# The 26 block products of the last group also for the group before it, its early sums on another engine, and some work around groups 0 and 1 moved

## The chip, the core and the metric

The kernel runs on one core of a Trainium2 chip. A core has five engines that each run their own list of instructions in order and wait for each other by semaphores: TensorE (PE in the profile: matmuls, with the weight loads of each shown apart as PEld), VectorE (DVE), ScalarE (ACT), GpSimd (POOL) and SyncE (SP), which here only issues DMAs, as POOL does in a few places. SBUF is the on-chip memory in which the operands lie, PSUM the banks that matmuls write, HBM the memory outside. The metric is the device time of one execution in microseconds (us). One execution was also taken by the hardware profiler; all views below are of that one.

## The reference

Everything is fp32. Attention in chunks of 64 tokens, then a layer that adds the real part of a two-dimensional Fourier transform, normalises each token, and sends it through two weight matrices, 512 to 2048 and back:

```python
# q, k, v: (8 batches, 8 heads, 576 tokens, 64)
scores = scale * np.matmul(q_c, k_c.transpose(0, 1, 2, 4, 3))     # per chunk of 64
attn = softmax(scores)
x = (attn @ v_c) -> (8, 576, 512)
u = x + np.real(np.fft.fft(np.fft.fft(x, axis=1), axis=2))
un = (u - mean(u)) / np.sqrt(var(u) + 1e-06)
ch = np.maximum(un @ w_ch1, 0.0) @ w_ch2                        # 512 -> 2048 -> 512
out = u + ch
```

## The kernel before

**Tiles and groups.** The 4608 tokens lie in 36 tiles of 128 rows. They are of three kinds: LO and HI, whose chunks are mirror images of each other in the Fourier step, and RE ("rest"), the odd chunks of two batches. Four tiles are a group, and there are nine: groups 0 to 7 are the LO and HI tiles of one batch each, group 8 is the four rest tiles. A group passes through an up phase (512 to 2048, with relu) and a down phase (2048 to 512, and u is added). Between the matmuls of one group stand, as side work, attention and Fourier of a later batch (`side`, L1487), and the normalising (`normed`, L983), transposing (`turned`, L1001) and combining (`combined`, L1019) of the next group's tiles.

**Fewer matmuls by sums of blocks.** Group 0 is computed plainly (`up_first` L1187, `down_plain` L1231: 64 matmuls of 128x512 in each phase). From group 1 on (`up_halves` L1266, `down_halves` L1320) each matrix product is cut into 2 x 2 x 2 blocks and made from seven block products in place of eight, whose operands are sums of blocks: 7 x 2 x 8 = 112 matmuls of 128x256 in a down phase. `combined` makes the sums of un, `operands` (L1167) those of the hidden values h1 for the down phase: two on VectorE and one on GpSimd for each of eight m, issued in the up phase behind the pair that made them. Group 8's down phase (`down_few`, L1386) is cut finer, into 4 x 4 x 2 blocks, and made from 26 products (the table PRODUCTS) of four matmuls of 128x256, 104 in all. Its first operands are sums of 128x512 blocks of h1, on GpSimd: the six of the list EARLY while the up phase is in its third pair of four, the others in down_few, next to the product that they follow (`sums`, L1180). It reads each product's result out of PSUM on VectorE.

**Sums of weights.** These are made once on the chip and kept in HBM. Up phases read s1 in slabs of 256 KB (ring of 10, L1157); halved down phases read s2 in slabs of 1 MB (ring of 3 in the tile wb, L1162); down_few reads 0.5 MB blocks, some of s2, most of s3 (L1160). s3 holds 19 sums. `make_rest` (L1110) makes them: for each of two halves it loads eight blocks (L1126), makes 23 sums of 128x512 on GpSimd (L1135) and stores 19 (L1142), in buffers that attention and Fourier need no longer. The main loop starts it when group 6 is in its down phase, takes the first real step five steps later, and leaves out every fourth step from group 7 on. A ring of 11 slabs for s3 is filled from two steps into group 8's up phase.

**Order.** All code stands under `tc.manual_schedule()`: every engine executes its instructions in the order in which the program text issues them. The main loop calls a step t of the running phase's generator, and then of the side work that is due by a count (`begin[g]`, `ready_at[g]`: the step in which group g+1's values must be there). An up phase of groups 1 to 8 has 16 steps, a down phase 14, down_few 13. SP's DMAs are issued in program order too. `FEW` (L1149) is the first group that uses down_few.

**Around groups 0 and 1.** In down_plain, the four tiles of group 1 are normed after m = 10, 10, 12, 12 and turned after m = 12, 13, 14, 14 of 16; the combined sums (L1028 to L1030) follow in the same step. At the end VectorE adds u to each result (L1251). Beside this, Fourier of batch 1 runs its last three mixes (L842), one of them for the rest rows. A mix goes to a bank of the tag "pt" (two of them), which the transposes use as well; the last mix of batch 1 goes to the tag "att" (one), which scores (`sc`, L449) use. VectorE reads a mix in L852 and L853.

Of the kernel before, what the change touches and what calls it, by code (L numbers as in the profile page):

```python
# [8 lines left out]
FP32 = mybir.dt.float32  # L9
# [7 lines left out]
def kernel(  # L17
# [32 lines left out]
    nc = tc.nc  # L50
# [3 lines left out]
    CH = 64  # L54
    NC = S // CH
    NM = 2
# [10 lines left out]
    G = 2 * NM  # L67
# [4 lines left out]
    one_p = ctx.enter_context(tc.tile_pool(name="one", bufs=1))  # L72
# [79 lines left out]
        "s24=s10-sb22", "s22=w-s10", "s25=w+s4", "s1=b21-s4", "s17=b21+b41", "s18=b12+b32", "s12=s18-s17", "s6=b42-s18",  # L152
    )
    STORED = tuple(text.split("=")[0] for text in MADE if text[0] == "s")
    NR2, NS3 = len(PRODUCTS), 11
    s3 = dram.tile([len(STORED), 128, Z3], FP32, name="s3")
    slab3 = [wb[:, i * Z3:(i + 1) * Z3].rearrange("p (m e) -> p m e", m=4) for i in range(6)]

# [634 lines left out]
    def fourier(b):  # L793
# [25 lines left out]
            yield  # L819
            z_joined()  # L820
        nc.scalar.copy(zs[0][0:1, 2], middle)
        if h == 1:
            z_rest(h)
        for i in range(NM):
            z_tile(zf, i)
        if h == 0:
            z_rest(h)
        yield

        def mixed(i):  # L830
            if (b, i) == (1, NM - 1):
                mix = ps_a.tile([128, 2, 512], FP32, tag="att", name="mix")[:, 0]
            else:
                mix = ps_t.tile([128, 512], FP32, tag="pt", name="mix")
            zt = zr.rearrange("p t h f -> p t (h f)") if i == NM else zf[:, :, 128 * i:128 * (i + 1)]
            for T, (cols, tab) in enumerate((
                (slice(0, HM + 1, 2), ce),
                (slice(1, HM, 2), co),
                (slice(0, DM, 2), cx),
                (slice(HM + 1, DM, 2), so),  # L840
            )):
                nc.tensor.matmul(  # L842
                    out=mix[:, cols], lhsT=zt[:, T], rhs=tab,
                    start=(T == 0), stop=(T == 3), skip_group_check=True,
                )
# [12 lines left out]
            eng = nc.gpsimd if kind(n) == HI else nc.vector  # L858
            eng.tensor_tensor(out=x[:, 0:w], in0=y[:, 0:w], in1=x[:, 0:w], op=ALU.add)

        for i in ((NM,) if h == 1 else ()) + tuple(range(NM)):
            y = both(*mixed(i))
            ns = [rests[b // 2]] if i == NM else [at[LO, b, i], at[HI, b, i]]
            for n in ns:
                added(y, n)
            means(ns)
            yield

    def fourier_early():
# [78 lines left out]
        for i in range(NM):  # L948
# [13 lines left out]
            if i == 0:  # L962
                normed(0, 1)
                turned(0, 0)
                keep_warm(1)
        put_off[2]()
        columns(1)
        normed(0, 2)
        turned(0, 2)
# [64 lines left out]
    def store(n, o):  # L1034

        last = n in groups[-1][1::2]
        for h, (b, c) in enumerate(chunks(n)):
            r0, t0 = h * CH, c * CH
            if kind(n) == LO:
                to = out[b, t0 + 1:t0 + CH + 1, :][::-1].rearrange("(i r) d -> r i d", r=2)[::-1]  # L1040
                nc.gpsimd.dma_start(out=to, in_=o[r0:r0 + CH])  # L1041
            elif kind(n) == RE:
                eng = nc.scalar if last and h else nc.sync
                eng.dma_start(out=out[b, t0 + 1:t0 + CH:2, :], in_=o[r0:r0 + ODD])
                eng.dma_start(out=out[b, t0 + 4:t0 + CH:2, :], in_=o[r0 + ODD + 2:r0 + CH])
                eng.dma_start(out=out[b, 0:t0 + 3:t0 + 2, :], in_=o[r0 + ODD:r0 + ODD + 2])
            else:
                for r in range(2):
                    nc.sync.dma_start(out=out[b, t0 + 1 - r:t0 + CH:2, :], in_=o[r0 + ODD * r:r0 + ODD * r + ODD])


# [58 lines left out]
    def make_rest():  # L1110
# [3 lines left out]
        z, spare = Z3 // 2, []  # L1114
        for i in range(4):
            spare.append(xall[:, 2 * G:2 * G + 4, :].rearrange("p a f -> p (a f)")[:, i * z:(i + 1) * z])
        for tag, n in (("q", 2), ("k", 2), ("zf", 2), ("two", 1), ("qT", 1), ("kT", 1), ("pT", 1)):
            t = one_p.tile([128, n * z], FP32, tag=tag, name="part")
            spare += [t[:, i * z:(i + 1) * z] for i in range(n)]
        last = {x: i for i, text in enumerate(MADE) for x in text.replace("=", "-").replace("+", "-").split("-")}  # L1120
        for half in range(2):
            part = slice(half * z, (half + 1) * z)
            where, behind = {}, []
            for name in ("b31", "b41", "b42", "b11", "b32", "d", "w", "b21"):
                where[name] = spare.pop(0)
                nc.sync.dma_start(out=where[name], in_=block_of(name)[:, part])  # L1126
                if half and name in ("b41", "b11", "d"):
                    yield
            yield
            for i, text in enumerate(MADE):  # L1130
                name = text.split("=")[0]
# [8 lines left out]
                while behind and (len(behind) > 3 or i == len(MADE) - 1):  # L1140
                    old = behind.pop(0)
                    nc.sync.dma_start(out=block_of(old)[:, part], in_=where[old])  # L1142
                    if last[old] <= i and old not in done_with:
                        done_with.append(old)
                spare += [where[x] for x in done_with if x not in behind]
                if i % 2:
                    yield

    FEW = NG - 1  # L1149
    first_of = {1: 1, 2: 1}  # L1150
    n_slab = {1: 0, 2: 0, 3: 0}

# [24 lines left out]
            return yall[:, i + 1].rearrange("p (m t) -> p m t", m=4)  # L1177
        return h1[:, 4 * j:4 * j + 4, i * 128:(i + 1) * 128]

    def sums(h1, texts):  # L1180

        for text in texts:
            out_, a, b, op = parsed(text)
            out_, a, b = (block_a(h1, x) for x in (out_, a, b))
            nc.gpsimd.tensor_tensor(out=out_, in0=a, in1=b, op=op)

    def up_first():  # L1187

# [42 lines left out]
    def down_plain(g, h1):  # L1231
# [4 lines left out]
        for m in range(KF):  # L1236
# [14 lines left out]
                    nc.vector.tensor_tensor(out=o, in0=dn, in1=natural(n), op=ALU.add)  # L1251
                    store(n, o)
            for j in range(G):
                if m == (10, 10, 12, 12)[j]:
                    normed(g + 1, j)
                if m == (12, 13, 14, 14)[j]:
                    turned(g + 1, j)
                    if j >= 2 and g + 1 >= first_of[1]:
                        joined.append((g + 1, j - 2))
# [6 lines left out]
    def up_halves(g):  # L1266
# [7 lines left out]
        for pair in range(HF // 2):  # L1274
            pas, pbs = {}, {}
            for turn_, o in enumerate(UP):
# [161 lines left out]
    with tc.manual_schedule():  # L1438
# [79 lines left out]
        for g in range(NG):  # L1518
            for _ in mlp(g):
# [108 lines left out]
```

## Time and profile before

| | us |
|---|---|
| runs | 1069.3, 1070.77, 1072.9 (median 1070.77) |
| profiled execution | 1069.92 |
| its span in the profile | 1068.1 |
| mean granted TensorE clock | 0.997 of full |

The times in the timeline count from the start of the span. In it, the phases begin on PE at:

| group | up phase | down phase |
|---|---|---|
| 0 | 52.0 | 115.8 |
| 1 | 192.5 | 252.0 |
| 2 | 310.2 | |
| 6 | 761.7 | 817.0 |
| 7 | 870.4 | 919.0 |
| 8 | 969.1 | 1017.4 |

The last matmul ends at about 1062.3; the last stores take the rest. An entry of the page's part 5 gives a line of the kernel, an engine, an operation with what it writes and reads, its count, the busy time, the mean duration in ns, and the idle time of the engine before it with what ended most of it. A row of the timeline gives start and length in us, and in brackets the idle time before it and what ended it. A row of the windows gives from:to, the length, the busy time of PE, PEld, DVE, ACT and POOL with the number of instructions, the granted clock of TensorE, the share of the 16 DMA engines, and GB/s.

### The profile page before, as it was taken

To read this page: it belongs to the slowest core of one execution; us is meant where nothing else is said; L and a number is where in the kernel's file an instruction comes from. 1 tells how busy PE (TensorE), PEld (TensorE's weight loads), DVE (VectorE), ACT (ScalarE), POOL (GpSimd) and SP (SyncE) were. 2 spreads that over 40 slices of the span, in tenths; PEclk is the share of its full clock that TensorE was granted. 3 is DMA by queue.
4 is the path that set the end of the run, shared out by engine and by line. 5 is a ranking of instruction groups with operands and counts; after the bars stand their busy time and mean duration, and the time that the engine had idled before them with its cause. 6 is when DMAs were issued, how large, how long until landed. Compare 5 with 4: busy or idle time off the path is not lost.

```text
span 1068.1 us, 20211 instructions
## 1 busy us (share of the span) xinstructions
PE 1046.5 (98%) x7498; PEld 855.5 (80%) x7498; DVE 612.2 (57%) x1321; ACT 315.5 (30%) x746; POOL 428.8 (40%) x561
## 2 busy tenths in 40 slices
PE   8999998899999999999999999999999999999997
PEld 6644454688888888888888888888888888888886
DVE  4798976874567465664565555745564545333331
ACT  4688563233113411322022312331133113101200
POOL 4310118853425241254134321624261656680281
PEclk9999999999999999999999999999999999999999
DMA  8767675686678547963687359835754569677663
GB/s 172 227 195 212 153 217 186 204 246 219 233 209 228 143 144 214 259 194 114 183 240 208 109 171 260 233 113 173 221 153 121 202 202 368 201 234 227 246 229 106
DMA packets 164351, 212.79 MB, mean 199 GB/s; under 512 B 76924, under 2 KB 110716, under 8 KB 157982
## 3 DMA queue, kind: packets, MB, share of 16 engines
q1 hardware_dynamic: 153436, 205.95, 63.6%
q0 software_dynamic: 9024, 4.91, 2.0%
q8 instruction: 59, 0.97, 0.4%
q10 hardware_dynamic: 1794, 0.66, 0.3%
q14 instruction: 38, 0.31, 0.1%
HBM read 177.31 MB, written 34.08 MB: 198 GB/s over the span
## 4 chain that ended last, share of the span: by engine, by line
PE 84%; DVE 5%; ACT 4%; DMA 3%; SPq 2%; issue 1%; POOL 0%; DVEq 0%; ACTq 0%; POOLq 0%
PE pa L1290 20%; PE pb L1342 18%; PE pb L1290 15%; PE pa L1342 14%; PE dn L1406 4%; PE pt L397 2%; PE xp L499 2%; DMA xall<-in_moe_w_ch_dram 2%; PE mix L842 2%; PE z L720 1%; SPq L263 1%; PE sc L449 1%; PE up L1197 1%; PE dn L1238 1%; DVE power L378 1%
## 5 line engine op out<-in xcount | busy, mean ns | idle before, releaser
L1290 PE MATMUL pa<-unT,wa 128*128 128x256 f32 x736 | 175.1, 381 | 0.0
L1290 PEld LDWEIGHTS pa<-unT,wa 128*128 128x128 f32 x736 | 138.2, 190 | 19.2
L1290 PE MATMUL pb<-wa 128*128 128x256 f32 x448 | 106.8, 381 | 0.0
L1342 PE MATMUL pa<-wb,h 128*128 128x256 f32 x448 | 101.5, 380 | 0.0
L1342 PE MATMUL pb<-wb,h 128*128 128x256 f32 x448 | 100.7, 379 | 0.0
L1290 PEld LDWEIGHTS pb<-wa 128*128 128x128 f32 x448 | 84.2, 190 | 11.9 <-DVE h L1300 0.4
L1342 PEld LDWEIGHTS pa<-wb,h 128*128 128x128 f32 x448 | 83.9, 190 | 11.3
L1342 PEld LDWEIGHTS pb<-wb,h 128*128 128x128 f32 x448 | 84.1, 190 | 11.0
L1171 POOL TENSOR_TENSOR h<-h 128x256 f32<-128x256 f32 x56 | 48.0, 865 | 110.2 <-DVE wb L1169 107.0
L1041 POOL DMA_DIRECT2D out_dram<-wb x28 | 18.8, 674 | 118.2 <-DVE wb L1359 82.1
L1296 DVE TENSOR_TENSOR wa<-pb,wa 128x256 f32<-128x256 f32 x56 | 23.8, 424 | 70.0 <-ACT wa L1295 70.0
L1290 PE MATMUL pb<-unT,wa 128*128 128x256 f32 x256 | 60.6, 380 | 1.3 <-DVE xall L1296 1.3
L1238 PE MATMUL dn<-wb,h 128*128 128x512 f32 x128 | 58.8, 609 | 0.0
L1304 ACT ACTIVATE h<-pa 128x256 f32<-128x256 f32 x64 | 24.5, 383 | 115.1 <-PE pa L1290 114.2
L1295 ACT COPY wa<-pa 128x256 f32<-128x256 f32 x56 | 20.8, 372 | 125.7 <-PE pa L1290 125.7
L1290 PEld LDWEIGHTS pb<-unT,wa 128*128 128x128 f32 x256 | 48.5, 190 | 8.6 <-POOL wb L1072 1.3
L1290 PE MATMUL pa<-wa 128*128 128x256 f32 x224 | 53.9, 383 | 0.0
L1310 ACT ACTIVATE h<-h 128x512 f32<-128x512 f32 x64 | 39.9, 629 | 41.3 <-DVE h L1309 41.0
L1342 PE MATMUL pb<-wb,yall 128*128 128x256 f32 x224 | 51.2, 381 | 0.0
L481 ACT COPY pT<-pt 128x512 f32<-128x512 f32 x36 | 20.9, 581 | 102.1 <-PE pt L397 101.8
L1342 PE MATMUL pb<-wb 128*128 128x256 f32 x224 | 50.7, 379 | 0.0
L1342 PE MATMUL pa<-wb,yall 128*128 128x256 f32 x224 | 50.5, 379 | 0.0
(302 smaller groups left out, 2025.5 us busy)
## 6 DMA issues: line engine op xcount, KB each, us to landing
wb<-s SPq DMA_DIRECT2D x49, 1024.0 KB, 5.2
wa<-s SPq DMA_DIRECT2D x196, 256.0 KB, 3.9
xall<-in_moe_w_ch_dram SPq DMA_DIRECT2D x22, 512.0 KB, 4.6
q<-in_q_dram SPq DMA_DIRECT2D x96, 112.0 KB, 3.8
k<-in_k_dram SPq DMA_DIRECT2D x96, 112.0 KB, 4.6
wb<-s SPq DMA_DIRECT2D x16, 512.0 KB, 4.9
v<-in_v_dram SPq DMA_DIRECT2D x124, 64.0 KB, 4.1
s<-part SPq DMA_DIRECT2D x30, 256.0 KB, 5.8
```

The source lines that it names most:

```text
L397: nc.tensor.transpose(pt[:, j, :], src(j), ident)
L481: nc.scalar.copy(t.rearrange("p j (c r i) -> p (j c) r i", c=2, r=2), pt.rearrange("p j (c i r) -> p (j c) r i", c=2, r=2)[:, :, ::-1])
L499: nc.tensor.matmul(out=xp[0][e][t0:t0 + CH, j * DV:(j + 1) * DV], lhsT=a[r0:r0 + CH, j, t0:t0 + CH], rhs=b[r0:r0 + CH, c, j, :], start=Tru ...
L842: nc.tensor.matmul(out=mix[:, cols], lhsT=zt[:, T], rhs=tab, start=(T == 0), stop=(T == 3), skip_group_check=True,)
L1171: nc.gpsimd.tensor_tensor(out=h1[:, m, hi], in0=h1[:, m, lo], in1=h1[:, m, hi], op=ALU.subtract)
L1238: nc.tensor.matmul(out=dn, lhsT=h1[:, m, s * 128:(s + 1) * 128], rhs=w2[:, m, :], start=(m == 0), stop=(m == KF - 1),)
L1290: nc.tensor.matmul(out=dst, lhsT=w[:, kk, r], rhs=rhs[o][:, kk], start=(o in (0, 1) and kk == 0), stop=(kk == 1), skip_group_check=True,)
L1296: nc.vector.tensor_tensor(out=b, in0=pbs[r][:, 0], in1=a, op=ALU.add)
L1304: nc.scalar.activation(out=h1[:, m, lo], in_=dst, func=ACTF.Relu)
L1310: nc.scalar.activation(out=h1[:, HF + m], in_=h1[:, HF + m], func=ACTF.Relu)
L1342: nc.tensor.matmul(out=dst, lhsT=lhs[:, m], rhs=w[:, m], start=(o in (0, 2) and m == 0), stop=(m == HF - 1), skip_group_check=True,)
L1406: nc.tensor.matmul(out=dst, lhsT=lhs[:, m], rhs=w[:, m], start=(fresh and not half and m == 0), stop=(m == 3), skip_group_check=True,)
```

## The change

1. `FEW = NG - 2`: groups 7 and 8 both use down_few. Group 7 has no `operands` any more and no 1 MB slabs; it reads 26 slabs of 0.5 MB.
2. The ring for s3 has 8 slabs in place of 11 (six in wb, two in the tags q and k). The first eight are fetched in the last four steps of group 7's up phase, two per step.
3. `make_rest` starts in the same step as before, and from then on takes one piece of work (two sums) in every step, with nothing left out; it has seven more buffers, asks for 13 of its 16 loads at the start, and for the others when buffers come free. What is left of it at the end of group 7's up phase is issued there.
4. The six EARLY sums of group 7 are on VectorE; those of group 8 stay on GpSimd, as do the sums inside down_few.
5. In Fourier the rest rows' part comes behind the others for every batch, and all mixes use the tag "pt".
6. The HI stores of group 0's results are put off: two per step, after group 1 has begun.
7. In down_plain, normed comes after m = 9, 9, 11, 11 and turned after m = 11, 12, 13, 13.

```diff
-    NR2, NS3 = len(PRODUCTS), 11
+    NR2, NS3 = len(PRODUCTS), 8
...
-        if h == 1:
-            z_rest(h)
         for i in range(NM):
             z_tile(zf, i)
-        if h == 0:
-            z_rest(h)
+        z_rest(h)
...
-            if (b, i) == (1, NM - 1):
-                mix = ps_a.tile([128, 2, 512], FP32, tag="att", name="mix")[:, 0]
-            else:
-                mix = ps_t.tile([128, 512], FP32, tag="pt", name="mix")
+            mix = ps_t.tile([128, 512], FP32, tag="pt", name="mix")
...
-        for i in ((NM,) if h == 1 else ()) + tuple(range(NM)):
+        for i in range(NM + h):
...
                 for r in range(2):
+                    if n in groups[0]:
+                        put_off.append((b, t0, r, o[r0 + ODD * r:r0 + ODD * r + ODD]))
+                        continue
                     nc.sync.dma_start(out=out[b, t0 + 1 - r:t0 + CH:2, :], in_=o[r0 + ODD * r:r0 + ODD * r + ODD])
...
-        for tag, n in (("q", 2), ("k", 2), ("zf", 2), ("two", 1), ("qT", 1), ("kT", 1), ("pT", 1)):
-            t = one_p.tile([128, n * z], FP32, tag=tag, name="part")
+        for pool, tag, n in (
+            (one_p, "q", 2), (one_p, "k", 2), (one_p, "zf", 2), (one_p, "two", 1), (one_p, "qT", 1), (one_p, "kT", 1),
+            (one_p, "pT", 1), (two_p, "ex", 1), (two_p, "ex", 1), (two_p, "pm", 1), (two_p, "pm", 1),
+            (three_p, "y", 1), (three_p, "y", 1), (three_p, "y", 1),
+        ):
+            t = pool.tile([128, n * z], FP32, tag=tag, name="part")
...
+        def take(keep):
+            while wanted and len(spare) > keep:
+                half, name = wanted.pop(0)
+                places[half][name] = spare.pop(0)
+                nc.sync.dma_start(out=places[half][name], in_=block_of(name)[:, half * z:(half + 1) * z])
+
+        take(8)
+        yield
...
                 spare += [where[x] for x in done_with if x not in behind]
+                take(7)
                 if i % 2:
                     yield
...
-    FEW = NG - 1
+    FEW = NG - 2
...
-    def sums(h1, texts):
+    def sums(h1, texts, eng=nc.gpsimd):
...
-            nc.gpsimd.tensor_tensor(out=out_, in0=a, in1=b, op=op)
+            eng.tensor_tensor(out=out_, in0=a, in1=b, op=op)
...
-                if m == (10, 10, 12, 12)[j]:
+                if m == (9, 9, 11, 11)[j]:
                     normed(g + 1, j)
-                if m == (12, 13, 14, 14)[j]:
+                if m == (11, 12, 13, 13)[j]:
                     turned(g + 1, j)
...
-                    sums(h1, EARLY.split()[turn_ - 1:turn_])
+                    sums(h1, EARLY.split()[turn_ - 1:turn_], nc.vector if g == FEW else nc.gpsimd)
...
-                if t == ready_at[NG - 3]:
+                if t == ready_at[FEW - 1]:
                     rest_ = make_rest()
-                    next(rest_)
-                if t > ready_at[NG - 3] + 4 and (t < begin[NG - 2] or t % 4 != 3):
+                if t >= ready_at[FEW - 1]:
                     next(rest_, None)
-                if t == begin[FEW] + 2:
-                    more = [xall[:, 2 * G:2 * G + 4, :].rearrange("p a f -> p (a f)")[:, i * Z3:(i + 1) * Z3] for i in range(2)]
-                    more += [one_p.tile([128, Z3], FP32, tag=tag, name="more") for tag in ("q", "k", "zf")]
-                    slab3.extend(a.rearrange("p (m e) -> p m e", m=4) for a in more)
-                if begin[FEW] + 2 <= t < begin[FEW] + 2 + NS3:
+                if t == begin[FEW] + 2 * HF - 1:
+                    for _ in rest_:
+                        pass
+                    slab3.extend(
+                        one_p.tile([128, Z3], FP32, tag=tag, name="more").rearrange("p (m e) -> p m e", m=4)
+                        for tag in ("q", "k")
+                    )
+                if begin[FEW] + 2 * HF - 4 <= t < begin[FEW] + 2 * HF:
                     fetch(3)
+                    fetch(3)
+                for _ in range(2 if t > begin[1] else 0):
+                    if put_off:
+                        b, t0_, r, o = put_off.pop(0)
+                        nc.sync.dma_start(out=out[b, t0_ + 1 - r:t0_ + CH:2, :], in_=o)
```

More of the change, by code (lines that the diff above doesn't have):

```diff
@@ L966, in fourier_early @@
         put_off[2]()
+        put_off.clear()
         columns(1)
@@ L1116, in make_rest @@
             spare.append(xall[:, 2 * G:2 * G + 4, :].rearrange("p a f -> p (a f)")[:, i * z:(i + 1) * z])
-        for tag, n in (("q", 2), ("k", 2), ("zf", 2), ("two", 1), ("qT", 1), ("kT", 1), ("pT", 1)):
-            t = one_p.tile([128, n * z], FP32, tag=tag, name="part")
+        for pool, tag, n in (
[4 more added lines that the diff above has]
+            t = pool.tile([128, n * z], FP32, tag=tag, name="part")
             spare += [t[:, i * z:(i + 1) * z] for i in range(n)]
         last = {x: i for i, text in enumerate(MADE) for x in text.replace("=", "-").replace("+", "-").split("-")}
-        for half in range(2):
[L1122 to L1129, printed above, removed]
+        places = [{}, {}]
+        wanted = [(half, name) for half in range(2) for name in ("b31", "b41", "b42", "b11", "b32", "d", "w", "b21")]
+        def take(keep):
[5 more added lines that the diff above has]
+        yield
+        for half in range(2):
+            part, where, behind = slice(half * z, (half + 1) * z), places[half], []
             for i, text in enumerate(MADE):
-                name = text.split("=")[0]
                 to = spare.pop(0)
```

## The prediction

> **What bounds the kernel.** First the page's busy table and slices: is one engine the limit, and everywhere?
>
> ```profile
> span 1068.1 us, 20211 instructions
> PE 1046.5 (98%) x7498; PEld 855.5 (80%) x7498; DVE 612.2 (57%) x1321; ACT 315.5 (30%) x746; POOL 428.8 (40%) x561
> PE   8999998899999999999999999999999999999997
> ...
> DMA  8767675686678547963687359835754569677663
> ```
>
> PE is busy in nine tenths or more of every slice from the ninth (214 us) to the last but one; in the chain of waits it holds 84%. So after 214 us only a removed matmul or a new PE wait can move the end. Its price is in the timeline of the last products:
>
> ```profile
> 1055.43 1.89 PE L1406 MATMUL dn<-wb,yall 128*128 128x256 f32 x8
> 1057.15 1.89 PE L1406 MATMUL dn<-wb,h 128*128 128x256 f32 x8
> 1058.88 1.89 PE L1406 MATMUL dn<-wb,yall 128*128 128x256 f32 x8
> 1060.61 1.89 PE L1406 MATMUL dn<-wb,h 128*128 128x256 f32 x8
> ```
>
> Each row is one product (four matmuls, two records each); starts lie 1.727 us apart, 0.432 a matmul, with no wait in brackets.
>
> **The eight matmuls.** Group 7's down phase goes from 7 x 2 x 8 = 112 matmuls (L1342) to 26 x 4 = 104 (L1406), both 128x256. Before, it began at 918.99 and group 8's up phase at 969.10. 8 x 0.432 = **-3.45 us**, all on the path, as PE never stops there.
>
> **The sums that leave and come in group 7's up phase.** operands() goes from it: 16 DVE and 8 POOL operations. They cost PE only one wait:
>
> ```profile
> L1290 PEld LDWEIGHTS pb<-wa 128*128 128x128 f32 x448 | 84.2, 190 | 11.9 <-DVE h L1300 0.4
> ```
>
> At 891.1 it left 0.24 us between matmuls; I take **-0.2**. In come six 128x512 sums on VectorE in the third pair. The DVE timeline around that wait, and POOL's, show what two-SBUF sums cost there:
>
> ```profile
> 889.08 1.25 DVE L1169 TENSOR_TENSOR wb<-h 128x256 f32<-128x256 f32 x1
> 890.36 1.37 DVE L1170 TENSOR_TENSOR yall<-wb,h 128x256 f32<-128x256 f32 x1
> ```
>
> ```profile
> 890.01 1.45 POOL L1135 TENSOR_TENSOR part<-part 128x512 f32<-128x512 f32 x1
> ```
>
> These DVE sums take 0.42 without a POOL sum beside them, but beside L1135 one waits for most of POOL's operation. The Trainium skill ("SBUF — State Buffer", section "Who interferes with whom") has the rule: one port pair goes whole to a GpSimd operation or to a DVE operation with two SBUF inputs, and the later one is blocked. It speaks against the change, which puts six such sums beside make_rest's POOL sums: at worst each costs its own 0.69 (L859 alone) plus a whole POOL operation, 1.27, so 6 x 1.96 = 11.8, and with the pair's ten evictions of 0.42, 16.0 us of DVE in a pair of 12.1 us of PE: +3.9. By the rows the added wait is 0.83 to 0.95 once each: 6 x 1.6 = 9.6 and 4.2, 13.8 against 12.1. But make_rest gives POOL two sums (2.5 us) a step of 3.0, and the sums come in six of seven turns, so DVE can run into the next turn without PE needing its bank. Ends 0 and +3.9; I take **0**, nearest the row above, where two long sums cost PE 0.24.
>
> **make_rest moves ahead.** Its 46 POOL sums (mean 1.289) start in the same step as before, now without pauses, two per step, and end in group 7's up phase, about 911, not at 961. POOL has room: 2.5 us of 3.0. What is behind it there is little; the first sum of down_few (a24) stands behind the last of them, and is not needed by the first product. In down phase 7 POOL has 23 sums of down_few, 23 x 1.27 = 29 us of 44.9; in group 8 it had as many, and PE never waited: 0. SP gets 13 loads of 256 KB at once ahead of the 1 MB slab for group 6's product 5. Loads landed 6.0 us after issue (part<-s), a 1 MB slab 5.2; 13 x 0.262 MB at the 389 GB/s below is 8.8 us, against about 14 us until that product. Ends 0 and +0.7; I take 0.1.
>
> **Slabs and the DMA rate.** This is the step that can turn the sign. The first eight half-MB slabs of group 7 are asked for in the last four up steps, and every later one when the product eight before it is done: 7 x 1.727 = 12.1 us ahead. In up phase 7 (48.4 us): 28 weight slabs x 0.262 = 7.3 MB, about 25 stores x 0.262 = 6.6, 8 slabs x 0.524 = 4.2: 18 MB, 373 GB/s on average. The windows show what this core's queues have carried:
>
> ```profile
> 880.00:890.00 10.00, 10.00 (x48) 8.81 (x47) 4.66 (x10) 2.84 (x6) 7.05 (x6) 1.00 1.03 389
> 890.00:900.00 10.00, 10.00 (x47) 8.49 (x46) 6.64 (x12) 3.27 (x8) 8.34 (x8) 1.00 1.04 389
> ...
> 1037.00:1047.00 10.00, 10.00 (x48) 8.80 (x47) 2.82 (x9) 0.00 (x0) 8.86 (x8) 1.00 0.83 308
> ```
>
> (last two columns: DMA share and GB/s). 389 with the engines full; the down phase of group 8 needs 0.524 / 1.727 = 304 and PE never waits. The Trainium skill ("DMA: Bandwidth & Descriptors", section "Where 436 GB/s comes from") says that HBM to SBUF transfers are bound near 358 GB/s. By it, 18 MB take 50.3 us, 1.9 more than the phase has; by the row 46.3, 2.1 less. The measured row decides, but with little left: the last of the eight land 8 to 10 us into a 12-us lead. Ends 0 and +6 (18 MB at 330); I take **+0.2**.
>
> **The early part, groups 0 and 1.** Here PE does wait:
>
> ```profile
> 171.12 0.65 PE L397 MATMUL pt<-ident,un 128*128 128x128 f32 x4 [1.84 <-ACT un L996]
> 173.75 0.84 PE L449 MATMUL sc<-kT,qT 64*64 64x64 f32 x32 [1.98 <-DVE y L853]
> ```
>
> ```profile
> 192.52 1.97 PE L1290 MATMUL pb<-xall,wb 128*128 128x256 f32 x8 [2.63 <-DVE o L1251]
> 198.89 1.97 PE L1290 MATMUL pb<-unT,wa 128*128 128x256 f32 x8 [0.96 <-DVE xall L1296]
> ```
>
> Behind the first two comes a stretch at half clock:
>
> ```profile
> 174.20:177.60 3.40, 3.40 (x23) 1.72 (x13) 3.04 (x7) 1.09 (x5) 3.32 (x3) 0.50 0.28 93
> ```
>
> It costs 3.40 x 0.5 = 1.7 us, and the four waits 7.4; with 0.5 of smaller ones 9.6 us in all. The change moves each. Normed and turned come one m (3.5 us) sooner, so the combining sums no longer stand before the eviction L1251: the 2.63 should become about 1.3. The transposes of un come sooner too, but their input still hangs on the DVE statistics of the last mixes, and on ScalarE the copy that frees the bank pt stands behind two un operations: the 1.84 becomes about 2.9, a second transpose waits 0.8, one more 0.3. The score matmul no longer waits for a bank that a mix held, but for a kT transpose (1.1) that now stands behind the combining sums: 1.98 becomes about 0.9. The three mixes of batch 1 now share pt, so the third waits until VectorE has read the second (L853 ends about 1.5 after the matmuls): 1.5 new. The 0.96 becomes 1.4. In all 9.1, if the waits, now spread, no longer bring the half clock; in the row it followed two waits of nearly 2 us within 4 us. So 9.1 against 9.6: I take **-0.4**. Ends: -4.3 (the 2.63 and the 1.7 go, nothing comes) and +1.8 (the new bank wait, nothing goes). The put-off stores of group 0 are two SP issues of 0.32 a step of 3.0, with no transfer due behind them: 0.
>
> **Sum.** -3.45 - 0.2 + 0.1 + 0.2 - 0.4 = -3.75 us. The profiled run took 1069.92 (span 1068.1 plus 1.8), so 1066.2; the median of the three runs is 0.85 above that, so **1067.0**.
>
> **Rivals.** *A, the forecast*, -3.7: PE dense, DMA at its row. 0.50. *B, the gain is eaten early or in small waits*: half clock stays (+1.7), first down products wait 0.7: about -1.4, 1069.4; for it, every early wait moves and none is plainly removed; against it, they hold 7.4 us that may shrink. 0.29. *C, slabs late (slower)*: if the queues carry under 330 GB/s in phase 7, stores of 256 KB (5.8 us to land) and fetches push the eight slabs past the phase, +6 or more, and with a ring of 8 at 304 GB/s needed nothing is caught up: 2.5 to 6 us slower, about 1074.5. It decides from about 340 GB/s down; for it, the share is 1.03 already, and many transfers are of 256 KB; against it, 389 held for 20 us. 0.17. *D, the DVE sums stop PE in the third pair*: +3.9 against -3.7, 1071. 0.04. That the change does nothing is excluded: 8 matmuls are gone.
>
> A 0.3% step is 3.2 us, about what a measurement can tell: the limits are 1067.6 and 1074.0. A lies just beyond the first, and part of its width within: **faster 0.42** (seven tenths of A, a quarter of B); same 0.41 (the rest of A and B, D); slower 0.17 (C). Range **1064.6 to 1072.8**: below, the early part's good end with a spread of the runs; above, B and D and the mild part of C.
>
> **And after it.** Down phase 7 ends with the combining sums of group 8 on VectorE after product 23, so 3.45 us stand for what group 8's first product reads; before, four products of 1.727, 6.9, stood. Four sums of 0.42 fit, beside a POOL sum (1.37 each) they do not all; at most a wait of 1, in B.
>
> **What would show it.** Down phase 7 44.9 us between its first and last products, no wait in brackets at L1406 (C: waits on DMA in its first products). Third pair: no PE wait on h (D). Around 174 a granted clock of 1.0 (else B). Group 1's first product at about 191.4 to 192.5. make_rest's last POOL sum before 920. I am wrong if SP holds the slabs back, or if a wait that I walked by hand in 160 to 200 us is double.

## The result, and the profile after

The changed kernel took 1065.93 us in the median of four runs (1065.14 to 1067.8); the kernel before, in the runs beside it, 1071.84 (1069.3 to 1073.22). The ratio is 0.9956, with an interval of 0.9939 to 0.9973. Twelve more runs, made beside later experiments, gave 1067.12 against 1069.99: 0.9974 (0.9960 to 0.9987). All runs of each kernel together, 16 of this one and 99 of before, have the medians 1067.03 and 1070.53: 3.5 us apart, where the forecast was 3.75. The forecast time was 1067.0.

The sum fits. Its terms do not all fit, as the profiled execution (1066.34, span 1064.5) shows. First the page:

```profile
span 1064.5 us, 20218 instructions
PE 1040.8 (98%) x7482; PEld 850.8 (80%) x7482; DVE 619.6 (58%) x1329; ACT 315.2 (30%) x744; POOL 443.1 (42%) x565
...
DMA  8767575777678446973687358934753759997265
```

PE is as dense as before, and has 16 records less (two per matmul). In the DMA row three nines now stand side by side: the slices from 878 to 958 us, most of group 7's up phase and its down phase (before: 9, 6 and 7 there). The timeline of PE at the start of that down phase:

```profile
917.05 3.62 PE L1412 MATMUL dn<-wb,h 128*128 128x256 f32 x16
920.50 3.62 PE L1412 MATMUL dn<-wb,yall 128*128 128x256 f32 x16
924.32 1.97 PE L1412 MATMUL dn<-wb,yall 128*128 128x256 f32 x8 [0.20 <-DMA wb<-s]
926.12 1.89 PE L1412 MATMUL dn<-wb,h 128*128 128x256 f32 x8
929.31 3.69 PE L1412 MATMUL dn<-more,h 128*128 128x256 f32 x16 [1.30 <-DMA more<-s]
```

(L1412 is the matmul of down_few, L1406 before.) The rows hold four products, then the fifth, the sixth, and the seventh with the eighth. The fifth and the seventh come late, each for a slab of weight sums, and each then needs some tenths more to get going: in all 1.98 us of the 3.45 that eight matmuls less are worth. The phases, read as the distances of the first products, add up so:

| from first to first product, us | before | after |
|---|---|---|
| group 0 up, to group 1 up | 140.54 | 138.79 |
| group 1 up, to group 6 down | 624.48 | 624.39 |
| group 6 down | 53.40 | 53.91 |
| group 7 up | 48.59 | 48.34 |
| group 7 down | 50.11 | 48.63 |
| group 8 up | 48.34 | 48.34 |

Early, 1.75 us are gained; there the stretch at half clock is missing. This is the row of the windows that stood at 0.50 before:

```profile
174.20:177.60 3.40, 3.40 (x41) 1.89 (x40) 3.30 (x6) 1.32 (x5) 3.32 (x3) 1.00 0.79 264
```

And the waits around it, from the timeline of PE:

```profile
161.97 0.46 PE L836 MATMUL mix<-ce,zr 128*128 128x129 f32 x2 [1.07 <-DVE y L847]
...
169.31 0.63 PE L397 MATMUL pt<-ident,un 128*128 128x128 f32 x4 [2.56 <-DVE y L847]
...
173.90 0.63 PE L397 MATMUL pt<-ident,un 128*128 128x128 f32 x4 [0.53 <-DVE y L847]
...
180.34 0.66 PE L397 MATMUL pt<-ident,un 128*128 128x128 f32 x4 [1.12 <-ACT unT L1006]
```

The mix of the rest rows waits for its bank (1.07), then the transposes wait for the same two banks (L847 is VectorE's last reading of a mix); the scores no longer wait at 174, and group 1's first product no longer waits for an eviction. One kernel's single profile can't say whether the missing half clock is the change's work or chance. So two questions were open: what the early part is worth on average, and why slabs came late at a DMA rate that seemed to suffice.

### The profile page after: what moved, and what is told of

It reads as the page before. It is cut to its first block, busy times and chain, and to the rows that moved or that the text cites. A ratio compares the mean times of both kernels' runs of the same rounds, so it can differ in the third digit from the quotient of the medians.

```text
span 1064.5 us, 20218 instructions
## 1 busy us (share of the span) xinstructions
PE 1040.8 (98%) x7482; PEld 850.8 (80%) x7482; DVE 619.6 (58%) x1329; ACT 315.2 (30%) x744; POOL 443.1 (42%) x565
## 4 chain that ended last, share of the span: by engine, by line
PE 82%; DVE 5%; DMA 4%; ACT 4%; SPq 3%; POOL 1%; issue 1%; DVEq 0%; ACTq 0%; POOLq 0%
PE pa L1296 19%; PE pb L1348 15%; PE pb L1296 14%; PE pa L1348 12%; PE dn L1412 7%; PE dn L1244 4%; PE pt L397 2%; PE mix L836 2%; PE z L720 2%; PE xp L499 2%; DMA wb<-s 1%; PE sc L449 1%; SPq L263 1%; DMA more<-s 1%; POOL part L1140 1%
## 5 line engine op out<-in xcount | busy, mean ns | idle before, releaser
L1348 PE MATMUL pa<-wb,h 128*128 128x256 f32 x384 | 87.2, 380 | 0.0
L1348 PE MATMUL pb<-wb,h 128*128 128x256 f32 x384 | 86.4, 379 | 0.0
L1177 POOL TENSOR_TENSOR h<-h 128x256 f32<-128x256 f32 x48 | 40.8, 857 | 98.9 <-DVE wb L1175 91.2
L1348 PEld LDWEIGHTS pa<-wb,h 128*128 128x128 f32 x384 | 71.8, 190 | 9.7
L1348 PEld LDWEIGHTS pb<-wb,h 128*128 128x128 f32 x384 | 72.0, 190 | 9.4
L1302 DVE TENSOR_TENSOR wa<-pb,wa 128x256 f32<-128x256 f32 x56 | 23.8, 425 | 68.9 <-ACT wa L1301 68.9
L1191 POOL TENSOR_TENSOR h<-h 128x512 f32<-128x512 f32 x34 | 42.5, 1266 | 27.7 <-ACT h L1316 22.8
L1412 PE MATMUL dn<-wb,h 128*128 128x256 f32 x224 | 50.5, 379 | 0.0
L1203 PE MATMUL up<-unT,wa 128*128 128x512 f32 x108 | 49.4, 598 | 0.0
```

Of the source, the lines that this page charges most:

```text
L1177: nc.gpsimd.tensor_tensor(out=h1[:, m, hi], in0=h1[:, m, lo], in1=h1[:, m, hi], op=ALU.subtract)
L1191: eng.tensor_tensor(out=out_, in0=a, in1=b, op=op)
L1203: nc.tensor.matmul(out=up, lhsT=w1[:, kk, m * 128:(m + 1) * 128], rhs=unT[:, kk], start=(kk == 0), stop=(kk == KD - 1), skip_group_check=True,
L1302: nc.vector.tensor_tensor(out=b, in0=pbs[r][:, 0], in1=a, op=ALU.add)
L1348: nc.tensor.matmul(out=dst, lhsT=lhs[:, m], rhs=w[:, m], start=(o in (0, 2) and m == 0), stop=(m == HF - 1), skip_group_check=True,)
L1412: nc.tensor.matmul(out=dst, lhsT=lhs[:, m], rhs=w[:, m], start=(fresh and not half and m == 0), stop=(m == 3), skip_group_check=True,)
```

## The experiments

Times are medians with the ratio to the runs of before that stand beside them; not every line of a longer edit is shown. "Theory" in the texts on record is the reading just given.

**before_again**: the kernel before, unchanged.

> The kernel before, unchanged, for a second profile of it. Theory (the early gain is the half clock's): the stretch at a granted clock of 0.5 behind the waits at 171 to 174 us is there again, and group 1 begins near 192.5. Rival (the half clock is chance): it is absent here, and group 1 begins 1.5 to 2 us earlier, near 190.7, without any change.

One run, 1068.56 us. The first half of the theory held: 0.5 again, this time from 171 to 174, behind waits of 0.80 and 1.98. The second did not: group 1 began at 190.34, as soon as in the changed kernel, since the whole execution had started its group 0 one us earlier, and one of the waits was a us shorter. Times from the start of the span don't compare; from here on distances between phases are used.

**early_only**: parts 5, 6 and 7 alone.

```diff
-            if (b, i) == (1, NM - 1):
-                mix = ps_a.tile([128, 2, 512], FP32, tag="att", name="mix")[:, 0]
...
+            mix = ps_t.tile([128, 512], FP32, tag="pt", name="mix")
...
-        for i in ((NM,) if h == 1 else ()) + tuple(range(NM)):
+        for i in range(NM + h):
...
-                if m == (10, 10, 12, 12)[j]:
+                if m == (9, 9, 11, 11)[j]:
-                if m == (12, 13, 14, 14)[j]:
+                if m == (11, 12, 13, 13)[j]:
...
```

> The kernel before with parts 5, 6 and 7 of the change alone (Fourier order and banks, stores put off, normed and turned one m sooner); group 7 stays with 112 matmuls. Theory: group 1 begins at 190.4 instead of 192.5 and nothing later moves: 2.1 us faster than before. Rival (the early gain is chance or given back later): 0 to 0.5 us.

1068.9 us against 1071.13: 0.9982 (0.9971 to 0.9992), so about 2 us faster, as the theory had it. But its profiled execution, its slowest run, had two stretches at half clock, at 171 and at 208, and from group 0's up phase to group 6's down phase it needed 4.7 us more than the changed kernel's. The gain is an average, not a fixed step.

**few_only**: parts 1 to 4 alone.

```diff
-    NR2, NS3 = len(PRODUCTS), 11
+    NR2, NS3 = len(PRODUCTS), 8
...
-    FEW = NG - 1
+    FEW = NG - 2
...
```

> The kernel before with parts 1 to 4 alone (26 products in group 7, the ring of 8, make_rest without pauses, early sums on VectorE); the early part stays as it was. Theory: 3.45 for the matmuls and 0.25 for operands, less 2.0 of slab waits in down phase 7 and 0.5 of a wait for un in down phase 6: 1.2 us faster. Rival (the forecast's own sizes, slab waits 0.3 in all): 3.4 us faster.

1068.27 us against 1071.13: 0.9972 (0.9961 to 0.9983), 2 to 4 us, nearer the rival's 3.4. The profile of it says what the theory said: group 6 down 54.07, group 7 up 48.35, down 49.09; the sum is 0.6 us under before. Its wait, in the timeline of PE (L1414 is the matmul of down_few here):

```profile
919.49 3.62 PE L1414 MATMUL dn<-wb,h 128*128 128x256 f32 x16
924.63 5.75 PE L1414 MATMUL dn<-wb,yall 128*128 128x256 f32 x24 [1.52 <-DMA wb<-s]
```

Here it is the third product that waits. So the waits are real, but differ in place and size from one execution to the next, and the runs on the whole did better than this one.

**slabs_ahead**: the changed kernel; the first two slabs of group 7, which are blocks of s2 and stored long before, are asked for in the first up step instead of the thirteenth.

```diff
-                if begin[FEW] + 2 * HF - 4 <= t < begin[FEW] + 2 * HF:
+                if t == begin[FEW] or begin[FEW] + 2 * HF - 3 <= t < begin[FEW] + 2 * HF:
                     fetch(3)
                     fetch(3)
```

> The changed kernel, with the first two s3-ring slabs of group 7 (both are blocks of s2, ready long before) asked for in the first step of its up phase in place of the thirteenth. Theory (the queues are full from 886 to 946 us, and 1 MB out of that stretch is 2.6 us of transfer): the waits on slabs in down phase 7 fall from 2.0 to under 0.5, 1.5 us faster than the changed kernel. Rival (not the rate: SP issues the last slabs late because it stands behind waits for the 256 KB ring, or the sums come late): the waits stay near 2.

1066.51 us against 1071.13: 0.9968 (0.9952 to 0.9984). The down phase took 46.65 us, with no wait on any slab: 1.98 less. But the megabyte now stood on SP ahead of the 256 KB slabs of the up phase, and one of these came late, as the timeline of PE shows:

```profile
886.04 1.89 PE L1296 MATMUL pa<-wa 128*128 128x256 f32 x8
888.92 1.97 PE L1296 MATMUL pb<-unT,wa 128*128 128x256 f32 x8 [0.99 <-DMA wa<-s]
```

That phase took 49.57 instead of 48.34. So the down phase's waits go when these bytes leave the crowd, and most of the wait only moved while they stayed in the queue before something urgent.

**slabs_hole**: the same two slabs, four steps before the end of group 6's down phase.

```diff
-                if begin[FEW] + 2 * HF - 4 <= t < begin[FEW] + 2 * HF:
+                if t == begin[FEW] - 4 or begin[FEW] + 2 * HF - 3 <= t < begin[FEW] + 2 * HF:
```

> The changed kernel, with the same two slabs asked for four steps before the end of group 6's down phase, where the DMA engines are at 0.3 of their time. Theory: as with slabs_ahead no wait on slabs in down phase 7 (before: 1.9 us), and now none on the 256 KB slabs in up phase 7 either (there: 1.0); up7 48.3 and down7 46.7 us from first to first product, 1.9 us faster than the changed kernel. Rival (SP's order, not the bytes): a wait of 1 us or more comes up somewhere else.

1066.79 us against 1070.74: 0.9962 (0.9949 to 0.9975). In the profile both phases came out as the theory had them: 48.35 and 46.65, span 1061.8. The windows of this kernel:

```profile
856.00:866.00 10.00, 9.92 (x48) 8.49 (x48) 8.38 (x11) 0.00 (x0) 7.62 (x8) 1.00 0.59 171
...
906.00:916.00 10.00, 10.00 (x48) 8.81 (x47) 3.67 (x9) 2.77 (x6) 3.56 (x4) 1.00 1.01 324
916.00:926.00 10.00, 10.00 (x48) 8.81 (x47) 3.67 (x10) 0.83 (x2) 8.71 (x8) 1.00 1.03 410
```

The first row, where the engines' share was 0.27 in the changed kernel, took the megabyte, and PE is busy all of the last two. The median did not follow: it is 0.2 us below the 1067.03 of all the changed kernel's runs, and the scatter of the runs (1064.3 to 1073.8) is larger than the 1.9 us. So what the 1.98 us are worth in the runs is not shown.

**early_pool**: the six early sums of group 7 on GpSimd.

```diff
-                    sums(h1, EARLY.split()[turn_ - 1:turn_], nc.vector if g == FEW else nc.gpsimd)
+                    sums(h1, EARLY.split()[turn_ - 1:turn_], nc.gpsimd)
```

> The changed kernel with the six early sums of group 7 on GpSimd, as group 8's are. Theory (POOL is full in up phase 7, and what it delays are the stores of weight sums and with them the slabs): make_rest ends 7.6 us later, and the waits on slabs in down phase 7 grow from 1.9 to 4 to 6 us: 2 to 4 us slower than the changed kernel. Rival (the place of these sums is of no account, POOL has room): same within 0.5 us, and slab waits near 2.

1068.75 us against 1070.74: 0.9983 (0.9974 to 0.9993). The runs stand 1.5 us nearer to before than the changed kernel's, less than the theory's 2 to 4, and the intervals overlap. The last sum of make_rest began at 914.6, in the changed kernel at 909.1: 4.6 us later when both are counted from the start of their up phase, not 7.6. Its slab waits are 2.2 us, within the 0.7 to 2.4 that profiles with the same slabs and these sums on VectorE show. The sizes of the theory fell; that VectorE is the better place is likely, not shown.

**turn_later**: the first tile of group 1 turned after m = 12.

```diff
-                if m == (11, 12, 13, 13)[j]:
+                if m == (12, 12, 13, 13)[j]:
```

> The changed kernel, with the first tile of group 1 turned after m = 12 as the second, instead of after 11; nothing else moves. Theory (the waits of 2.6 and 0.5 us before its transpose at 169 us are for the DVE chain of the last mix, not for un): with one m of matmuls between, they go, and at most 0.5 to 1 comes elsewhere: group 1 begins 2 us sooner, counted from the first product of group 0's up phase. Rival (the DVE chain itself sets when group 1 can begin): the wait only moves to the next transpose; no gain.

1066.67 us against 1070.74: 0.9957 (0.9946 to 0.9969), five runs, no better than the changed kernel. The rival held, as the timeline shows: the first transpose waits for nothing, the second for all.

```profile
170.57 0.60 PE L397 MATMUL pt<-ident,un 128*128 128x128 f32 x4
174.46 1.09 PE L397 MATMUL pt<-ident,un 128*128 128x128 f32 x4 [3.29 <-DVE y L847]
```

Two transposes one after the other need both banks of pt, and one of them is free only when VectorE has read the last mix.

**fourier_only**: part 5 alone. (Part 7 alone, normed_only, gave no time, so its share stays open: normed after m = 9 needs the statistics of tiles whose mix comes a step later in the old order.)

> The kernel before with part 5 alone (rest rows' mix last, all mixes in the bank pt). Theory (parts 5 and 7 work together): the wait of 1.98 us for the scores' bank goes, one of 1 to 1.6 us for pt comes before the third mix, the wait of 2.6 us before group 1's first product stays, since the combining sums still stand before the eviction: 0 to 0.7 us faster. Rival (part 5 is the whole early gain): 1.5 to 2 us faster.

1068.74 us against 1069.99: 0.9990 (0.9981 to 0.9999), 0.1 to 2 us faster. Its waits are those of the theory: none for the scores, 1.59 for the mix's bank, 1.09 for un, 3.00 for the eviction. The distance to group 1 is 138.46, though, 1 to 2 us less than in the two profiles of before, because no stretch at half clock lies in it; in this execution it comes right after.

**after_again**: the changed kernel, unchanged.

> The changed kernel, unchanged, for more runs and a second profile beside the next ones. Theory (its gain is a sum of a surer part in group 7's down phase and of rarer half clock early): 4 to 5 us faster than before in the median, waits on slabs in down phase 7 between 1 and 2 us again. Rival (the first four runs were lucky): 2 to 3 us.

1067.12 us against 1069.99, 2.9 us: the rival's size, so the first four runs stood lower than the rest. The slab waits of this profile are 0.73 us, less than expected, and early it had the half clock twice. The windows that cover both:

```profile
169.90:173.30 3.40, 3.40 (x8) 1.85 (x8) 2.22 (x5) 0.80 (x4) 3.40 (x3) 0.50 0.00 0
207.40:210.80 3.40, 3.37 (x38) 2.80 (x39) 3.06 (x10) 1.15 (x2) 2.29 (x2) 0.50 0.74 237
```

**before_warm**: the kernel before, with dummy matmuls in front of group 1's first transpose.

```diff
-    def turn(src):
+    def turn(src, warm_up=0):
...
+        for j in range(warm_up):
+            nc.tensor.matmul(out=pt[:, j % 4, :], lhsT=ident, rhs=ident, start=True, stop=True)
         for j in range(4):
             nc.tensor.transpose(pt[:, j, :], src(j), ident)
...
-        pt = turn(lambda j: un[:, j * 128:(j + 1) * 128])
+        pt = turn(lambda j: un[:, j * 128:(j + 1) * 128], 14 if (g, s) == (1, 0) else 0)
```

> The kernel before, with 14 added 128x128 matmuls of the identity into the bank of group 1's first transpose, which the transposes then overwrite: PE is busy in most of the 1.84 us in which it waited for un there. Theory (two waits of nearly 2 us within 4 us bring the stretch at half clock): the stretch becomes rarer, the mean granted clock rises from 0.9958 to above 0.997, and the kernel is about 1 us faster although it does more. Rival (the half clock does not hang on that wait): clock and time as before, or slower by the added work.

1070.58 us against 1069.99: 1.0007 (0.9997 to 1.0016). The first half of the theory held, the second fell. The timeline and the window of its profile:

```profile
168.88 3.29 PE L397 MATMUL pt<-ident 128*128 128x128 f32 x28
172.00 0.60 PE L399 MATMUL pt<-ident,un 128*128 128x128 f32 x4
173.46 0.69 PE L451 MATMUL sc<-kT,qT 64*64 64x64 f32 x32 [0.85 <-DVE y L855]
...
192.07 3.55 PE L1292 MATMUL pb<-xall,wb 128*128 128x256 f32 x8 [4.12 <-DVE o L1253]
```

```profile
192.00:195.40 3.40, 3.33 (x8) 2.71 (x9) 3.33 (x9) 0.00 (x0) 3.17 (x6) 0.51 1.01 295
```

Around 174 the clock stays whole; the wait at 192, longer than before (4.12 us), now brings the half clock. That covering one wait passed the loss on to the next is not shown, though: few_only has the old early part without the dummies, and its one stretch at half clock lies at 192 too. The mean granted clock of the runs was 0.9966, against 0.9962 of before beside them, and the time was no shorter; more than that this run doesn't tell.

**hole_pause** and **hole_pause_2**: slabs_hole, and make_rest leaves out its sixth step, the one beside `combined` in group 6's down phase; the same kernel twice.

```diff
-                if t >= ready_at[FEW - 1]:
+                if t >= ready_at[FEW - 1] and t != ready_at[FEW - 1] + 6:
```

> The changed kernel with two slabs fetched four steps before the end of group 6's down phase, and with make_rest leaving out its sixth step, the one beside the combining sums. Theory: no slab wait in down phase 7 (1.9 before) and no wait for un in down phase 6 (0.3 to 0.5 before): 2 us faster than after_again, 6 us faster than before. Rival (what is taken off PE's waits there is made up for elsewhere): phases as short, but the median not below after_again by more than 0.5.

> hole_pause unchanged, for more runs and a second profile. Theory (its late part is at its floor): down phase 6, up phase 7 and down phase 7 take 53.4, 48.3 and 46.7 us again, while the start of group 1 and the number of stretches at half clock differ from the first profile; 4 to 5.5 us faster than before in the median. Rival (the short phases of the first profile were luck, as the changed kernel's slab waits of 2.0 and 0.7 us differ by execution): a wait on a slab or on un is back in one of the three phases.

1065.83 us against 1069.99 (0.9968, 0.9956 to 0.9980, five runs), and 1066.56 against 1070.39 (0.9963, 0.9949 to 0.9977, twelve runs). The wait it is meant to take away is one on un. In the changed kernel, VectorE's and then PE's timeline:

```profile
854.50 1.32 DVE L1023 TENSOR_TENSOR wa<-unT 128x256 f32<-128x256 f32 x1
855.85 1.40 DVE L1024 TENSOR_TENSOR wa<-unT,wa 128x256 f32<-128x256 f32 x1
857.18 1.49 DVE L1025 TENSOR_TENSOR unT<-unT 128x256 f32<-128x256 f32 x1
```

```profile
859.60 0.63 PE L397 MATMUL pt<-ident,un 128*128 128x128 f32 x4 [0.31 <-DVE un L993]
```

and in hole_pause, VectorE at the same place:

```profile
856.89 1.09 DVE L1023 TENSOR_TENSOR wa<-unT 128x256 f32<-128x256 f32 x1
858.01 0.43 DVE L1024 TENSOR_TENSOR wa<-unT,wa 128x256 f32<-128x256 f32 x1
858.36 0.42 DVE L1025 TENSOR_TENSOR unT<-unT 128x256 f32<-128x256 f32 x1
```

Without a sum of make_rest beside them on POOL, two of the three sums are short again and un is in time. In the kernel before POOL was empty at that place, and all three took 0.41 to 0.42; POOL's next row there is a store that waits:

```profile
860.60 0.71 POOL L1041 DMA_DIRECT2D out_dram<-wb  x1 [9.81 <-DVE wb L1359]
```

Both profiles have 53.41, 48.35 and 46.65 for the three phases: no wait is left in the late part. Over all 17 runs the median is 1066.27, against 1067.03 for the changed kernel's 16 and 1070.53 for before: clearly faster than before, and ahead of the changed kernel by 0.8 us, less than the 2 us expected and less than these runs can tell apart.

## Why the prediction was right

The forecast of 3.75 us less stands beside 3.5 over all runs. That the number came so close is partly luck. In the profile of after the late part (down phase 6 and both phases of group 7) gave 1.22 where the forecast had 3.35, because slabs were late and make_rest dearer, and the early part gave 1.84 where it had 0.4; the remaining 0.6 of the span's 3.6 lie ahead of group 0 and behind the last matmul. By its own steps:

- **The eight matmuls, -3.45.** Right. With no wait in it, down phase 7 takes 46.65 us in four executions (slabs_ahead, slabs_hole and both of hole_pause), against 50.11: 3.46.
- **operands, -0.2.** Right, 0.1: up phase 7 takes 48.34 to 48.35 in all five profiles with 26 products in group 7 and unmoved slabs; in five of kernels with the old group 7 it takes 48.34 to 48.65, 48.47 on average.
- **Early sums on VectorE, 0.** Right, though close. Beside POOL they took 0.96 to 1.75 us, and VectorE was busy for 9.49 of the 10 us from 896 to 906; PE did not wait. Two rows from the timelines of VectorE and POOL show the longest pair:

```profile
901.51 1.75 DVE L1191 TENSOR_TENSOR yall<-h 128x512 f32<-128x512 f32 x1
```

```profile
901.00 1.72 POOL L1140 TENSOR_TENSOR part<-part 128x512 f32<-128x512 f32 x1
```

  The price of one was a whole POOL operation at most once in six, nearer the row used for the forecast (1.6) than the rule's worst case (1.96).
- **make_rest ahead, +0.1.** The size was too small and the cause named was the wrong one. The loads never held up group 6's slabs. What cost 0.1 to 0.7 us (53.52 to 54.07 for down phase 6 in the seven profiles with make_rest unpaused, 53.40 before) were the POOL sums beside `combined`. The forecast has make_rest's sums start in the same step as before. Only its loads do: the old kernel waited five steps between the loads and the first sums, the changed one goes on at once, and its first sum begins 23.8 us into down phase 6 instead of 28.8. So POOL, empty beside `combined` before, now has sums there. The forecast had the port collision in its hands, applied it to the six early sums only, and did not ask which other VectorE sums the earlier sums would lie beside.
- **Slabs, +0.2.** This is the term that was mis-sized: 1.98 in the profile of after, and 0.73, 1.6, 2.2 and 2.4 in four other executions with the same slabs. The forecast took 18 MB for the phase and 389 GB/s for the queues. The phase carried 328 GB/s, 15.9 MB, and so left some 2 MB, four slabs, over. In its last 30 us the engines were full, and the rate was 356; it went above 389 only behind that, exactly while PE waited (windows of the changed kernel):

```profile
886.00:916.00 30.00, 30.00 (x141) 26.41 (x140) 16.52 (x31) 8.45 (x20) 23.97 (x18) 1.00 1.01 356
916.00:926.00 10.00, 9.80 (x46) 8.34 (x45) 3.20 (x8) 1.45 (x3) 8.02 (x7) 1.00 1.04 404
926.00:936.00 10.00, 8.70 (x41) 7.37 (x40) 2.90 (x7) 0.00 (x0) 8.11 (x7) 1.00 1.03 416
```

  An average over the whole phase hid that 866 to 876 moved only 212 GB/s, while the slabs could not be asked for before 906: what could not be carried in the first third had to come in the last. The forecast also took it for granted that all eight slabs are asked for in the up phase. Before each of slabs 3 to 8 SP stood for 0.3 to 2.0 us until an earlier transfer had landed, and the seventh, for which PE then waited, went out 3.2 us into the down phase:

```profile
920.21 1.83 SPq L1166 DMA_DIRECT2D more<-s  x2
```

  That is what the forecast named as a sign of being wrong, that SP holds the slabs back. It isn't a cause of its own: in hole_pause the seventh slab was asked for 4.3 us into the phase, and PE did not wait for it. By the page "DMA: Bandwidth & Descriptors" of the Trainium skill (section "Where 436 GB/s comes from") the limit for such transfers is some 358 GB/s, by which the forecast would have been 2 us worse, near the measured wait. The 356 of the crowded 30 us agree with it; the 404 to 416 behind them, on this core, the only one in use, do not. Why the rate was lower first was not tried.
- **The early part, -0.4.** Near in the average, but not step by step. From group 0's up phase to group 6's down phase, the profiles of before and of the kernels with its early part took 764.8 to 765.1 us (before, before_again, before_warm, few_only); the eight with the changed one took 762.3 to 768.1, on average 764.65. That is 0.3 less, but with a spread of 6; fourier_only, with part 5 alone, stands at 763.45. The many runs of early_only put it at 0.9 to 3.1, and what lies between is not settled. The waits walked by hand were 2.9, 0.8, 0.3 and 0.9, with 1.5 for the bank and 1.4 behind; measured 2.56, 0.53, 1.12, 0.85, 1.07 and 1.41; the 1.3 left for group 1's first product was none at all. The one thing not walked is a wait of the scores for a transpose of k at 205 to 208 (none to 3.04 us), whose input, a load of SP's, landed late; with it came the second half-clock stretch of early_only and after_again. It came with the change: six of the nine profiles with the new order of normed have it, none of the other five. The put-off stores stand behind this load on SP, so they are not what delays it. SP needed 1.3 to 3.6 us to issue the third of its four parts in eight of the nine, 0.42 to 0.48 in the five; why was not tried.
- **The half clock** was treated as one event, gone or not gone. It differs from execution to execution. The five profiles with the old order of normed have one stretch each, at 171 to 177 or behind the wait at 191 to 192; the nine with the new one have none (three), one (three) or the time of two (three). That is one on average in both, so the profiles don't show it rarer. The runs, which give their mean granted clock, do: (1 - clock) x 1066 is 4.2 us on average over the 94 runs of before beside the experiments, 2.7 over the 77 of the kernels with parts 5 to 7 as the change has them. (Some 1 us of each is the time behind the last matmul, at 0.5 in every profile.) So about 1.5 us less are lost. How much of the gain this is stays open: early_only's runs lost 1.1 us less than those beside them and were 2.2 faster, and one run of the changed kernel took 1069.6 us at a mean clock of 1.00.

Rival B had the right kind of events in it, small waits on slabs and the half clock staying, at odds of 0.29; in the first profile the early part gained more than the walk through the trace allowed, which made up for it. C, slabs late by 6 us, did not come: the waits ended by about the tenth product. D did not come: no wait on h stands in the third pair.

## What to carry to other kernels

Before a stretch is declared to have room in its DMA queues, divide it: bytes that can't be asked for before a certain point must fit behind that point, and a quiet window ahead of it is worth nothing unless some of them can be asked for there. When work on one engine is moved ahead or loses its pauses, look through every operation on the others that used to lie beside an empty engine. And where a kernel's runs scatter by 5 us, one profile of each version decides about a step only by distances inside it; what differs by chance shows only in several.

## What the runs showed of the hardware

A wait of PE of 2 to 4 us did not always bring the half clock: the 2.56 us wait before the first transpose is in after, after_again and early_pool alike, and only after_again of these ran the matmuls behind it at 0.50. When it came it lasted 3.41 us, or twice that once (turn_later, 173 to 180 us), which is 1.7 us of full clock each time. The page "TensorE: Matmul & The Clock Gate" of the Trainium skill (Part 1) describes the gate as a free-running window of about 3.4 us, so that the same kernel is caught or not by where the window lies; these rows agree.

The traces even show which wait is caught. Each of the 14 traces lists when the granted clock changes; all these times lie whole steps of 3.413 us behind the first entry of the list, and that entry comes 4.1 to 7.5 us into the span, elsewhere in each execution. Cut into such steps, 4334 in all, the profiles separate cleanly: PE was idle for 2.22 us or more in the step ahead of each of the 13 stretches, and no step with 2.03 us or less was followed by the start of one; where between the two the limit lies is not shown. Three steps around the wait at the first transposes:

```profile
166.46:169.87 3.41, 0.85 (x3) 0.12 (x2) 1.04 (x3) 2.15 (x6) 0.39 (x2) 1.00 0.77 271
164.88:168.29 3.41, 1.86 (x5) 0.55 (x3) 0.01 (x1) 3.16 (x10) 1.41 (x2) 1.00 1.04 360
168.94:172.36 3.42, 1.39 (x7) 0.94 (x8) 2.27 (x5) 0.98 (x3) 1.39 (x1) 1.00 0.37 128
```

The first is after_again's: the wait lies whole in one step, PE is busy for 0.85 us of it, and the half clock follows. In after (the second row) a border divides the same wait, and in slabs_ahead (the third) 1.39 us are busy: both stay at full clock. So a wait of 2.6 us costs itself alone or 1.7 us more, by where a border falls, and two waits of 0.8 and 2.0 us can add up within a step, as in before_again. An estimate from the same profiles, with the steps laid at every possible offset and over 2.1 us idle counted as caught: 1.0 caught step for an execution with the old order of normed, 0.65 for one with the changed early part, which is 0.6 us of the 1.5 by which the runs' clocks differ.

The DMA engines carried 404 to 418 GB/s over 10 us windows of mostly 512 KB reads (slabs_hole and after, 916 to 936 us), at a share of 1.03 to 1.04, and 356 over the 30 us before, in which 19 of the 41 transfers issued were stores of 256 KB, at 1.01.
